# Gate rows written in 64 byte pieces, and a backward pass that gives engines and the DMA path one operation at a time

## The chip, the core and the metric

The kernel runs on one core of one Trainium2 chip. The core has TensorE (PE, matrix products into PSUM banks), VectorE (DVE), ScalarE (ACT), GpSimd (POOL) and SyncE (SP). In this kernel SP issues the loads, POOL most stores to scratch in DRAM. The metric is the device time of one execution in microseconds (us), lower is better. Before the change it was 880.47 us, the median of three runs (879.82 to 882.48).

## The reference

An input x of 2,048 tokens by 640 features goes through two branches, and a gate per token mixes them:

```
g = sigmoid((x * gate_w).sum(-1))              # one number per token
a = Cr @ (x @ Wre.T) - Ci @ (x @ Wim.T)        # Fourier mixing over features and tokens
b = mish(x @ w1 + b1) @ w2                     # 640 -> 1728 -> 640
out = g * a + (1 - g) * b
```

All is float32.

## The kernel before

**Products.** Every float32 operand is split into a high part (rounded by ACT) and a low part (the rest, by DVE), and a product of two operands is three matmuls: high by high, high by low, low by high (`mm3`). On top of that, the large products are cut into 2 x 2 blocks and done with seven block products in place of eight, with sums of blocks before and after them. A class `Problem` does one such product in three steps, `first`, `second` and `third`. The sums of inputs, and the sums that bring results out of PSUM, are DVE `tensor_tensor` operations (`tt`, L259); ACT copies between PSUM and SBUF (`copy`, L268); operands of 128 x 512 are split at L286 (ACT) and L287 (DVE), weight blocks at L280 and L281; the matmul itself is L292.

**Stages.** The work runs in this order on PE:

1. `seq`, four problems q0 to q3: x by the cosine and the sine matrix over tokens. Results `u0` to `u9` go to DRAM.
2. `hid`, two problems: u by the feature matrices `wd_re`, `wd_im`. Results, multiplied by g, go to DRAM as `y`.
3. `dense`: x by w1, mish, multiplied by 1 − g for half of the tokens, to DRAM as `act`.
4. `fin`, two problems: act by w2, plus y, to the output.

Some problems put partial sums of their first step aside in DRAM (`ps`, `ph`, `po`) and load them again in the second. Loads are L246, stores L255.

**The gate.** `gates()` (recorded in the third seq problem) loads `gate_w` to all partitions and x in 16 tiles of 128 tokens by 640. One DVE operation per tile multiplies and sums over the features (L746) and leaves a column of `gcol`, a tile of 128 partitions by 16 columns. ACT takes the sigmoid (L750), and DVE makes `qcol` = 1 − g (L751). Later stages need g and 1 − g along the free dimension, the same on all partitions. So both tiles go out to DRAM as rows of 2,048 numbers, `grow` and `qrow` (L753), and pieces of 512 of a row are loaded again, broadcast to 128 partitions (`f<-grow`, `f<-qrow`, L246). In the row of before token k · 128 + p stands in column k of partition p, so neighbours in the row lie on different partitions and the store goes out in pieces of one number.

**The order.** No engine's order is written by hand. Every operation is first recorded in a `Graph`, with its engine, what it reads and writes, and a modelled duration. The order of PE is that of recording, and each matmul's time `op.at` is its place in it times 0.2267 us (`MM`). `wants()` gives every other operation a latest time, `want`: a pass backwards over the operations takes, for each, the earliest `want` of those that need it, less its own duration and 0.15 us (`HOP`). Operations that bring results out of PSUM (`prompt`) also have a time from a pass forward, and the earlier one holds. `run()` then simulates the engines and writes out, on each engine, the ready operation with the earliest `want` for which buffers are to be had. Five pools hand out the buffers: 8 PSUM banks, 10 operand pairs R, 18 tiles FS (`f`), 6 wide tiles X (`x`), 26 weight pairs W (`w`). A buffer is kept free for operations of earlier `want` (`v.ask`). SP and POOL share one modelled DMA path of 385 GB/s with a delay of 1.95 us. What comes out is a fixed order per engine; on the chip an engine goes through its list and stops at each operation until what it needs is there. That holds for SP too: a load that waits for a free tile, or for data in DRAM to land, stops every load behind it.

Of the kernel before, what the change touches and what calls it, by code (L numbers as in the profile page):

```python
# [14 lines left out]
S, D, F = 2048, 640, 1728  # L15
P = 128
N = 512
TG = S // N
KS = S // P
# [5 lines left out]
NR, NFS, NX, NW = 10, 18, 6, 26  # L25
MM = 0.2267
HOP, PROMPT, LATER, AHEAD = 0.15, 2.0, 8.0, 5.0


class Val:  # L30
# [15 lines left out]
class Graph:  # L46
# [35 lines left out]
    def wants(self):  # L82

        for op in self.ops:
            for d in op.deps:
                d.after.append(op)
            if op.engine == "PE":
                op.ends = op.at + op.took
                op.want = op.at
                continue  # L90
            op.prompt = op.psum or not op.fills and any(d.prompt and d.engine in ("ACT", "DVE") for d in op.deps)
            if op.prompt:
                op.ends = max([d.ends for d in op.deps if d.prompt or d.engine == "PE"], default=0) + op.took
                op.want = op.ends + (PROMPT if op.psum else LATER)
        for op in reversed(self.ops):
            late = min([a.want for a in op.after], default=1e9) - op.took - HOP
            op.want = late if op.want is None else min(op.want, late)

    def run(self, pools, rate, delay):

        self.wants()
        for op in self.ops:
            for v in op.vals:
                if v.pool and (v.ask is None or op.want < v.ask[0]):
                    v.ask = op.want, op.n, id(v)
        for p in pools:
            p.asks = sorted({v.ask for op in self.ops for v in op.vals if v.pool is p})
            p.soon = sorted({v.ask for op in self.ops if op.prompt for v in op.vals if v.pool is p and v.ask[1] == op.n})
        missing = {op.n: len(op.deps) for op in self.ops}
        free = {e: 0.0 for e in ("PE", "ACT", "DVE", "SP", "POOL")}  # L110
        ready = {e: [] for e in free}
        pe = [op.n for op in self.ops if op.engine == "PE"][::-1]
        for op in self.ops:
            if not missing[op.n]:
                insort(ready[op.engine], (op.want, op.n))
        events, now, left, dma = [], 0.0, len(self.ops), 0.0

        def granted(op, blocked):
            for v in op.vals:
                if v.pool and v.t is None:  # L120
                    if v.pool in blocked:
                        return False
                    p, n = v.pool, bisect_left(v.pool.asks, v.ask)
                    if not op.prompt:
                        n += bisect_left(p.soon, (v.ask[0] + AHEAD,)) - bisect_left(p.soon, v.ask)
                    if len(p.free) <= n:
                        blocked.add(v.pool)
                        return False
            return True

        while left:
            began = False
            for e, line in ready.items():
                if free[e] > now + 1e-9 or not line:
                    continue
                if e == "PE":
                    i = next((i for i, x in enumerate(line) if x[1] == pe[-1]), None)
                    if i is not None and not granted(self.ops[pe[-1]], set()):
                        i = None
                else:  # L140
                    blocked = set()
                    i = next((i for i, x in enumerate(line) if granted(self.ops[x[1]], blocked)), None)
                if i is None:
                    continue
                op = self.ops[line.pop(i)[1]]
                if e == "PE":
                    pe.pop()
                for v in op.vals:
                    if v.pool and v.t is None:
                        v.pool.asks.remove(v.ask)  # L150
                        if v.ask in v.pool.soon:
                            v.pool.soon.remove(v.ask)
                        v.t = v.pool.free.pop(0)
                op.emit()
                free[e] = now + op.hold
                if e in ("SP", "POOL"):
                    dma = max(now + delay, dma) + op.took - delay
                    end = dma + 0.1
                else:
                    end = now + op.took + 0.03  # L160
                heapq.heappush(events, (end, op.n))
                left -= 1
                began = True
            if began:
                continue
            times = [t for e, t in free.items() if t > now + 1e-9 and ready[e]]
            if events:
                times.append(events[0][0])
            assert times, ("stuck", left, pe and self.ops[pe[-1]].at, [(p.name, len(p.free)) for p in pools])
            now = max(now, min(times))  # L170
            while events and events[0][0] <= now + 1e-9:
                op = self.ops[heapq.heappop(events)[1]]
                for v in op.vals:
                    v.left -= 1
                    if not v.left and v.pool:
                        p = v.pool
                        p.free.append(v.t)
                        if p.heir and not p.asks:
                            p.heir.free += [p.part(t) for t in p.free]
                            p.free = []  # L180
                for a in op.after:
                    missing[a.n] -= 1
                    if not missing[a.n]:
                        insort(ready[a.engine], (a.want, a.n))
# [8 lines left out]
def fnet_mish_gate(ctx: ExitStack, tc: tile.TileContext, xn, xt, c_re, c_im, wd_re, wd_im,  # L193
                   w1a, w1b, b1a, b1b, w2, gw, out):
    nc = tc.nc
# [9 lines left out]
    R = Pool("r", [pair(f"r{i}", N) for i in range(NR)])  # L205
# [31 lines left out]
        return G.add("ACT", emit, r, w, took, took - 0.096)  # L237

    def dma(queue, emit, r, w, size):
        return G.add(queue, emit, r, w, 1.95 + size / 385e3, 0.605 if queue == "SP" else 1.0)  # L240

    ISSUE = {"SP": nc.sync, "POOL": nc.gpsimd}

    def load(pool, src, of=None, rows=P, cols=N, queue="SP"):
        v = Val(pool)
        dma(queue, lambda: ISSUE[queue].dma_start(v.t[:rows, :cols], src() if callable(src) else src),  # L246
            whole(of) if of else [], whole(v), rows * cols * 4)
        return v
# [113 lines left out]
    class Problem:  # L362
# [154 lines left out]
        def end(self):  # L517
            (p0, p1), t, h = self.b, self.t1, N // 2
            f, g = Val(FS), Val(FS)
            copy(f, p0)  # L520
            self.finish(2, t, f, "SP")
            for eng, c in (("ACT", slice(0, h)), ("DVE", slice(h, N))):
                def emit(c=c, eng=eng):
                    if eng == "ACT":
                        nc.scalar.activation(g.t[:, c], p1.t[:, c], AF.Copy)
                    else:
                        nc.vector.tensor_copy(g.t[:, c], p1.t[:, c])
                (act if eng == "ACT" else dve)(emit, whole(p1), [(g, eng)], h)

                def send(c=c, eng=eng):  # L530
                    o = out[3 * P:4 * P, t * N + c.start:t * N + c.stop]
                    (nc.scalar if eng == "ACT" else nc.sync).dma_start(o, g.t[:, c])
                G.add("ACT" if eng == "ACT" else "SP", send, [(g, eng)], [], 2.3, 0.1)

    once = {}

# [204 lines left out]
    def gates():  # L741

        wide = load(X, gw.partition_broadcast(P), cols=D)
        for k in range(KS):
            x = load(X, xn[k], cols=D)
            dve(lambda k=k, x=x: nc.vector.scalar_tensor_tensor(  # L746
                x.t, x.t, 1.0, wide.t, op0=OP.mult, op1=OP.mult, accum_out=gcol.t[:, k:k + 1]),
                whole(x, wide), whole(x) + [(gcol, k)], D, 0.1)
        cols = [(gcol, k) for k in range(KS)]
        act(lambda: nc.scalar.activation(gcol.t, gcol.t, AF.Sigmoid), cols, cols, KS)  # L750
        dve(lambda: nc.vector.tensor_scalar(qcol.t, gcol.t, -1.0, 1.0, op0=OP.mult, op1=OP.add), cols, whole(qcol), KS)  # L751
        for c, row, r in ((gcol, grow, cols), (qcol, qrow, whole(qcol))):
            dma("SP", lambda c=c, row=row: nc.sync.dma_start(row.t.rearrange("o (k p) -> p (o k)", p=P), c.t),  # L753
                r, whole(row), 1 << 18)
        act(lambda: nc.scalar.preload_act_table_set("mish"), cols, whole(table), 0, 1.0)

# [54 lines left out]
    for p in ou:  # L811
        p.second(fin.low)
        p.third()
    G.run([psum, R, FS, X, W], 385.0, 1.95)


# [40 lines left out]
```

## Time and profile before

| | |
|---|---|
| median of 3 runs | 880.47 us |
| the profiled execution | 882.19 us, of it the span 880.4 us |
| PE busy | 861.5 us, 98% of the span, 3,772 matmuls |
| DVE busy | 677.8 us, 77%, 1,213 instructions |
| ACT busy | 461.6 us, 52%, 849 instructions |
| POOL busy | 69.3 us, 8% |
| moved by DMA | 203.50 MB in 107,071 packets, mean 231 GB/s |
| packets under 512 B | 16,640 |

How to read the views: a row of a table of groups or a timeline names the engine, the line of the kernel, the operation and `out<-in` by the program's names without buffer numbers (`f<-u` is a load of a u block into an FS tile). Times are us from the start of the span. `SPq` is SP's queue of issued DMAs; the time to landing is from the issue until the data is there. "Waited for" tables name the waiting engine and line, then what ended the wait, then the total, the number of waits and the longest. The windows view has one row per stretch of time: its length, busy time and count of PE, weight loads, DVE, ACT and POOL, the granted clock of PE (1.00 is full), the busy share of the 16 DMA engines, and GB/s. A digit in the DMA line is the busy share of one fortieth of the window in tenths.

### The profile page before, as it was taken

To read this page: it belongs to the slowest core of one execution; us is meant where nothing else is said; L and a number is where in the kernel's file an instruction comes from. 1 tells how busy PE (TensorE), PEld (TensorE's weight loads), DVE (VectorE), ACT (ScalarE), POOL (GpSimd) and SP (SyncE) were. 2 spreads that over 40 slices of the span, in tenths; PEclk is the share of its full clock that TensorE was granted. 3 is DMA by queue.
4 is the path that set the end of the run, shared out by engine and by line. 5 is a ranking of instruction groups with operands and counts; after the bars stand their busy time and mean duration, and the time that the engine had idled before them with its cause. 6 is when DMAs were issued, how large, how long until landed. Compare 5 with 4: busy or idle time off the path is not lost.

```text
span 880.4 us, 11973 instructions
## 1 busy us (share of the span) xinstructions
PE 861.5 (98%) x3772; PEld 710.2 (81%) x3772; DVE 677.8 (77%) x1213; ACT 461.6 (52%) x849; POOL 69.3 (8%) x132
## 2 busy tenths in 40 slices
PE   9999999999999999999995999999999999999998
PEld 7888888888888888888884888888888888887786
DVE  7899957866785667997976999924666997739891
ACT  7675535535453445674552576745655755522541
POOL 0000001002000200011001102111111100000000
PEclk9999999999999999999997999999999999999999
DMA  9796939555954755559975959565444687526943
GB/s 319 273 337 223 324 123 366 181 204 164 346 191 146 254 202 179 196 200 367 374 193 154 373 179 338 211 222 190 146 159 188 214 304 265 199 77 221 366 160 119
DMA packets 107071, 203.50 MB, mean 231 GB/s; under 512 B 16640, under 2 KB 19072, under 8 KB 107008
## 3 DMA queue, kind: packets, MB, share of 16 engines
q1 hardware_dynamic: 96752, 169.57, 56.5%
q0 software_dynamic: 10112, 33.04, 10.0%
q8 instruction: 29, 0.48, 0.2%
q14 instruction: 34, 0.28, 0.1%
q10 hardware_dynamic: 144, 0.13, 0.0%
HBM read 164.40 MB, written 38.29 MB: 230 GB/s over the span
## 4 chain that ended last, share of the span: by engine, by line
PE 85%; DMA 6%; DVE 6%; ACT 1%; issue 1%; SPq 0%; ACTq 0%; DVEq 0%
PE ps L292 85%; DMA f<-u 4%; DVE f L259 3%; DMA x<-in_xn_dram 1%; DMA f<-po 1%; DVE x L746 1%; DVE x L259 0%; DVE r8l L287 0%; ACT f L268 0%; DVE r9l L287 0%; DMA out_dram<-f 0%; ACT r8h L286 0%; DVE r1l L287 0%; DVE r5l L287 0%; ACT r1h L286 0%
## 5 line engine op out<-in xcount | busy, mean ns | idle before, releaser
L259 DVE TENSOR_TENSOR f<-f,f 128x512 f32<-128x512 f32 x316 | 211.8, 686 | 19.6 <-DMA f<-u 15.3
L268 ACT ACTIVATE f<-ps 128x512 f32<-128x512 f32 x129 | 74.5, 595 | 40.2 <-PE ps L292 35.1
L259 DVE TENSOR_TENSOR f<-ps,f 128x512 f32<-128x512 f32 x92 | 59.8, 684 | 38.4 <-PE ps L292 38.3
L255 POOL DMA_DIRECT2D u<-f x40 | 21.5, 540 | 321.6 <-DVE f L259 310.3
L286 ACT ACTIVATE r4h<-f 128x512 fp32r<-128x512 f32 x40 | 25.2, 629 | 37.9 <-PE ps L292 20.2
L286 ACT ACTIVATE r6h<-f 128x512 fp32r<-128x512 f32 x40 | 25.3, 631 | 37.5 <-PE ps L292 17.3
L286 ACT ACTIVATE r1h<-f 128x512 fp32r<-128x512 f32 x39 | 24.5, 629 | 33.0 <-PE ps L292 17.7
L550 ACT ACTIVATE f<-f,b1s 128x512 f32<-128x512 f32 x36 | 25.6, 722 | 28.2 <-DVE f L259 28.1
L286 ACT ACTIVATE r3h<-f 128x512 fp32r<-128x512 f32 x41 | 25.8, 629 | 26.0 <-PE ps L292 13.1
L286 ACT ACTIVATE r2h<-f 128x512 fp32r<-128x512 f32 x41 | 25.8, 628 | 25.4 <-PE ps L292 16.6
L286 ACT ACTIVATE r9h<-f 128x512 fp32r<-128x512 f32 x42 | 26.4, 629 | 23.1 <-PE ps L292 10.7
L255 POOL DMA_DIRECT2D act<-f x52 | 28.2, 542 | 131.0 <-DVE f L259 65.3
L286 ACT ACTIVATE r5h<-f 128x512 fp32r<-128x512 f32 x40 | 25.1, 629 | 25.3 <-PE ps L292 13.3
L287 DVE TENSOR_TENSOR r3l<-f,r3h 128x512 fp32r<-128x512 f32 x41 | 28.2, 688 | 11.6 <-ACT r3h L286 11.2
L286 ACT ACTIVATE r8h<-f 128x512 fp32r<-128x512 f32 x39 | 24.5, 629 | 24.0 <-PE ps L292 14.8
L286 ACT ACTIVATE r0h<-f 128x512 fp32r<-128x512 f32 x40 | 25.1, 629 | 22.1 <-PE ps L292 13.9
L287 DVE TENSOR_TENSOR r9l<-f,r9h 128x512 fp32r<-128x512 f32 x42 | 28.9, 688 | 9.6 <-ACT r9h L286 9.0
L287 DVE TENSOR_TENSOR r0l<-f,r0h 128x512 fp32r<-128x512 f32 x40 | 27.5, 688 | 11.4 <-ACT r0h L286 11.3
L287 DVE TENSOR_TENSOR r2l<-f,r2h 128x512 fp32r<-128x512 f32 x41 | 28.2, 688 | 10.0 <-ACT r2h L286 9.7
L287 DVE TENSOR_TENSOR r8l<-f,r8h 128x512 fp32r<-128x512 f32 x39 | 26.8, 688 | 11.3 <-ACT r8h L286 11.0
L287 DVE TENSOR_TENSOR r6l<-f,r6h 128x512 fp32r<-128x512 f32 x40 | 27.5, 688 | 9.7 <-ACT r6h L286 9.4
L287 DVE TENSOR_TENSOR r5l<-f,r5h 128x512 fp32r<-128x512 f32 x40 | 27.5, 688 | 9.2 <-ACT r5h L286 8.9
(1827 smaller groups left out, 2650.0 us busy)
## 6 DMA issues: line engine op xcount, KB each, us to landing
f<-in_c_re_dram SPq DMA_DIRECT2D x128, 256.0 KB, 4.9
f<-in_c_im_dram SPq DMA_DIRECT2D x128, 256.0 KB, 3.5
f<-act SPq DMA_DIRECT2D x84, 256.0 KB, 5.2
f<-u SPq DMA_DIRECT2D x80, 256.0 KB, 5.7
act<-f POOLq DMA_DIRECT2D x52, 256.0 KB, 2.9
f<-in_xt_dram SPq DMA_DIRECT2D x44, 256.0 KB, 4.4
u<-f POOLq DMA_DIRECT2D x40, 256.0 KB, 5.2
x<-in_xn_dram SPq DMA_DIRECT2D x25, 320.0 KB, 5.7
```

Source lines behind the costliest of these rows:

```text
L255: dma(queue, lambda: ISSUE[queue].dma_start(d.t, v.t[:rows]), whole(v), whole(d), rows * N * 4)
L259: dve(lambda: nc.vector.tensor_tensor(o.t[rows, x], a.t[rows, y], b.t[rows, z], op=op), whole(a, b), whole(o), n)
L268: act(lambda: nc.scalar.activation(o.t, a.t, AF.Copy, scale=scale), whole(a), whole(o))
L286: act(lambda: nc.scalar.activation(r.t[0][:, :N], src.t[:, :N], AF.Copy), whole(src), [(r, 0)])
L287: dve(lambda: nc.vector.tensor_tensor(r.t[1][:, :N], src.t[:, :N], f32(r.t[0][:, :N]), op=OP.subtract), whole(src) + [(r, 0)], [(r, 1)])
L292: G.add("PE", lambda: nc.tensor.matmul(bank.t, w.t[wn][:, k * P:k * P + P], x.t[xn_][:, :N], start, stop, skip_group_check=True), [(w, (k, ...
L550: act(lambda: nc.scalar.activation(o.t[rows], src.t[rows], AF.Mish, **more), whole(src, table) + whole(b1s) * bias, whole(o), more=0.1)
L746: dve(lambda k=k, x=x: nc.vector.scalar_tensor_tensor(x.t, x.t, 1.0, wide.t, op0=OP.mult, op1=OP.mult, accum_out=gcol.t[:, k:k + 1]), whol ...
```

## The change

Two parts.

The gate's x is read so that partition p has the 16 tokens p · 16 to p · 16 + 15, one per tile; then the 16 columns of a partition are neighbours in the row, and the store of a row has 128 pieces of 16 numbers (64 bytes). The number of instructions is the same.

```
+        tokens = xn.rearrange("k p d -> (k p) d").rearrange("(p k) d -> k p d", k=KS)
         for k in range(KS):
-            x = load(X, xn[k], cols=D)
+            x = load(X, tokens[k], cols=D)
...
-            dma("SP", lambda c=c, row=row: nc.sync.dma_start(row.t.rearrange("o (k p) -> p (o k)", p=P), c.t),
+            dma("SP", lambda c=c, row=row: nc.sync.dma_start(row.t.rearrange("o (p k) -> p (o k)", k=KS), c.t),
```

The backward pass of `wants()` is replaced. The new one keeps a heap of operations all of whose successors are done, and takes the latest first. On ACT and on DVE, and on the DMA path that SP and POOL share, operations may not overlap: each must end before the one taken ahead of it begins (`back`). A matmul's `want` is `op.at` alone. The model of the DMA path becomes 370 GB/s with a delay of 2.2 us, and a transfer holds the path for its bytes' time (`op.moves`). Where an operation takes two buffers of one pool, its `v.ask` is set so that both count from the time of the later (the loop added to `run`).

```
+DELAY, RATE = 2.2, 370e3
...
-        for op in reversed(self.ops):
+        back, todo, line = {}, {op.n: len(op.after) for op in self.ops}, []
+
+        def reached(op):
             late = min([a.want for a in op.after], default=1e9) - op.took - HOP
-            op.want = late if op.want is None else min(op.want, late)
-
-    def run(self, pools, rate, delay):
+            if op.want is not None:
+                late = op.at if op.engine == "PE" else min(op.want, late)
+            heapq.heappush(line, (-late, -op.n))
+        for op in self.ops:
+            if not op.after:
+                reached(op)
+        while line:
+            late, n = heapq.heappop(line)
+            op, late = self.ops[-n], -late
+            if op.engine == "PE":
+                op.want = late
+            else:
+                e, held = ("DMA", op.moves) if op.engine in ("SP", "POOL") else (op.engine, op.hold)
+                ends = min(late + op.took, back.get(e, 1e9))
+                op.want, back[e] = ends - op.took, ends - held
+            for d in op.deps:
+                todo[d.n] -= 1
+                if not todo[d.n]:
+                    reached(d)
...
+        for op in self.ops:
+            for v in op.vals:
+                if v.pool and v.ask[1] == op.n:
+                    also = [u.ask[0] for u in op.vals if u.pool is v.pool and u is not v]
+                    if also:
+                        v.ask = min(v.ask, (max(also), op.n, id(v)))
...
-                    dma = max(now + delay, dma) + op.took - delay
+                    dma = max(now + DELAY, dma) + op.moves
...
-        return G.add(queue, emit, r, w, 1.95 + size / 385e3, 0.605 if queue == "SP" else 1.0)
+        op = G.add(queue, emit, r, w, DELAY + size / RATE, 0.605 if queue == "SP" else 1.0)
+        op.moves = size / RATE
+        return op
...
-                G.add("ACT" if eng == "ACT" else "SP", send, [(g, eng)], [], 2.3, 0.1)
+                G.add("ACT" if eng == "ACT" else "SP", send, [(g, eng)], [], 2.3, 0.1).moves = 0.4
```

The matmuls and their order, the number of instructions of every kind, and the pools stay as they are.

More of the change, by code (lines that the diff above doesn't have):

```diff
@@ L94, in wants, with run @@
                 op.want = op.ends + (PROMPT if op.psum else LATER)
-        for op in reversed(self.ops):
+        back, todo, line = {}, {op.n: len(op.after) for op in self.ops}, []
+        def reached(op):
             late = min([a.want for a in op.after], default=1e9) - op.took - HOP
-            op.want = late if op.want is None else min(op.want, late)
-    def run(self, pools, rate, delay):
+            if op.want is not None:
[17 more added lines that the diff above has]
+                    reached(d)
+    def run(self, pools):
         self.wants()
@@ L813, in fnet_mish_gate @@
         p.third()
-    G.run([psum, R, FS, X, W], 385.0, 1.95)
+    G.run([psum, R, FS, X, W])
 def kernel(**inputs):
```

## The prediction

> **What bounds the kernel now.** I read the page's first rows, then the waits of PE (TensorE), then windows around its largest wait, then the queues in those windows. Page, first rows:
>
> ```profile
> span 880.4 us, 11973 instructions
> ## 1 busy us (share of the span) xinstructions
> PE 861.5 (98%) x3772; PEld 710.2 (81%) x3772; DVE 677.8 (77%) x1213; ACT 461.6 (52%) x849; POOL 69.3 (8%) x132
> ```
>
> PE is busy for all but 880.4 − 861.5 = 18.9 us. The matmuls and their order do not change, so the change can win only what PE stands idle or runs slowly, and can lose any amount. The waits of PE (us in total, times, longest):
>
> ```profile
> PE ps L292 <- DVE f L259: 10.3, 1, 10.3
> PE ps L292 <- ACT ps L268: 2.2, 3, 1.5
> ```
>
> One wait holds 10.3 us: a PSUM bank that DVE has not yet emptied. Windows around the large wait (width; busy us and count of PE, PEld, DVE, ACT, POOL; granted clock; DMA share; GB/s):
>
> ```profile
> 442.00:457.00 15.00, 15.00 (x68) 12.40 (x67) 10.59 (x19) 8.66 (x16) 0.00 (x0) 1.00 0.72 163
> 457.00:470.50 13.50, 13.50 (x60) 10.88 (x58) 5.71 (x12) 1.60 (x3) 0.00 (x0) 1.00 0.66 120
> 470.50:480.80 10.30, 0.02 (x1) 0.01 (x1) 9.38 (x17) 4.65 (x8) 0.76 (x2) 0.69 0.48 178
> 480.80:485.00 4.20, 4.17 (x10) 3.32 (x11) 4.20 (x8) 0.60 (x1) 2.95 (x6) 0.53 0.79 276
> ```
>
> PE starves at 470.5 because DVE was short of input before it: 5.71 us busy of 13.5. After the wait PE runs on at a clock of 0.53. What DVE waited for between 442 and 476, and what the DMA engines did from 440 to 472 (40 slices of 0.8 us):
>
> ```profile
> DVE f L259 <- DMA f<-u: 12.9, 4, 7.1
> ```
>
> ```profile
> DMA  9999999950259443379888799982131366585989
> GB/s 377 398 387 394 381 394 242 87 2 0 20 41 69 26 38 26 32 129 312 335 271 182 156 320 394 303 56 22 1 0 8 31 61 36 28 69 82 318 318 402
> DMA packets 6996, 5.40 MB, mean 169 GB/s; under 512 B 4443, under 2 KB 4443, under 8 KB 6994
> ```
>
> Twice the path falls from nearly 400 GB/s to a few tens for some 9 us, and of 6,996 packets 4,443 are small. SP's issues show which they are (start, issue us; the rows between are left out), and the table of issues gives the landing times (KB each, median us):
>
> ```profile
> 442.10 0.37 SPq L753 DMA_DIRECT2D grow<-gcol  x1
> ...
> 457.44 0.37 SPq L753 DMA_DIRECT2D qrow<-qcol  x1
> ```
>
> ```profile
> f<-u SPq DMA_DIRECT2D x80, 256.0 KB, 5.7
> ...
> out_dram<-f SPq DMA_DIRECT2D x1, 128.0 KB, 1.9
> b1s<-in_b1a_dram SPq DMA_DIRECT2D x1, 6.5 KB, 5.2
> ...
> grow<-gcol SPq DMA_DIRECT2D x1, 8.0 KB, 11.9
> qrow<-qcol SPq DMA_DIRECT2D x1, 8.0 KB, 11.1
> ```
>
> Each gate row (8 KB, 2,048 pieces of 4 B, 4,096 of the small packets) takes 11 to 12 us. The chain that ended last has the loads issued right behind the rows:
>
> ```profile
> 442.77 12.22 DMA f<-u
> ...
> 457.86 13.29 DMA f<-u
> ```
>
> They take 12.22 and 13.29 us against a median of 5.7: 6.5 and 7.6 late, 14.1 together. That is about DVE's 12.9 us of waiting, which becomes PE's 10.3.
>
> **The change part by part.**
>
> *Rows in 64 B pieces.* Removed per row: 1,920 of 2,048 pieces; the instruction count stays. No row of before shows 128 pieces of 64 B going out. Nearest is b1a's load, 128 pieces of 52 B: 5.2 us. Ends: 1.9 (the 128 KB store of the quiet end) and 11.9 (no gain). I take 5.2; by it a piece costs (11.9 − 5.2)/1,920 = 3.5 ns, and 128 of them 0.4 us: no load behind is held measurably.
>
> The Trainium skill, "DMA: Bandwidth & Descriptors" (Specifications), says that pieces under 512 B miss line rate because the engine reads, modifies and writes; 64 B is still under that, as 4 B was. If that alone made the row slow, it would take 11.9 us again and the sum would be the third rival's; the section on one DMA's anatomy fits about 2.0 us plus bytes by 436 GB/s, an estimate of 2.0 us for 8 KB, and with it the sum below stands.
>
> *What goes with it.* DVE's 12.9 us disappear if the loads come at their usual 5.7. DVE's release of the bank, which let PE go on at 480.8, then comes at about 480.7 − 12.9 = 467.8, before the 470.5 at which PE wants the bank. Slack: 2.7 us, not much. Gain 10.3 us. With it goes the slow clock: nine matmuls of 0.43 us in place of 0.2267 us (starts of 480.82 to 484.77 below, less the first one's 0.57), 9 × 0.2 = 1.8, call it 1.9.
>
> ```profile
> 480.82 0.76 PE L292 MATMUL ps<-r4h,w11h 128*128 128x512 f32 x1 [10.30 <-DVE f L259]
> ...
> 484.77 0.39 PE L292 MATMUL ps<-r5h,w21h 128*128 128x512 f32 x1
> ```
>
> The Trainium skill, "TensorE: Matmul & The Clock Gate" (Part 1), has the clock halve after an idle window of about 3.4 us and come back after about as long busy; the 0.53 of 480.8 to 485 agrees. By it a wait that shrinks under 3.4 us would cost its own length only, and one that stays above would keep the 1.9.
>
> *Gathering the gate's x rows.* Partition p now takes tokens 16p to 16p+15: still 128 pieces of 2,560 B, from addresses 40,960 B apart rather than adjacent. Sixteen loads, taken at nothing; were each 1 us of path longer, 16 us would fall into 396 to 442, where the path is full (next fence), and the sums of u would be late.
>
> *The planner.* PE's list is the same. In the written-out orders 932 of DVE's 1,195 operations, 522 of ACT's 849, 448 of SP's 643 and 7 of POOL's 128 change place. Three moves matter. (a) Five loads of `wd_re` (320 KB, tops of the hidden stage), which SP issues at 78 to 83 us, go out at about 370 to 384, with their splits on ACT and DVE. (b) Eight loads of u go ahead of the gate's x loads, from about 398–412 to 360–383. (c) The grow row's first read stands directly behind its store, so SP stops until the row has landed; behind it wait two u loads, the qrow store and the next reads. Before, three loads went in between, and SP stopped 4.2 us:
>
> ```profile
> SPq L246 <- DVE w14l L281: 19.9, 3, 10.4
> ...
> SPq L246 <- DMA grow<-gcol: 4.2, 1, 4.2
> ```
>
> With a landing of 5.2 SP stops about 5 us from some 443, and is free at 448; before, the same loads were issued from 449 to 455. So (c) costs nothing, and with 11.9 us it would cost what before paid. For (a) and (b), windows with more and less room:
>
> ```profile
> 346.00:396.00 50.00, 50.00 (x223) 41.38 (x222) 48.00 (x99) 35.47 (x74) 2.78 (x6) 1.00 0.63 215
> 396.00:442.00 46.00, 46.00 (x204) 38.07 (x203) 40.73 (x80) 23.99 (x45) 4.20 (x8) 1.00 1.02 371
> ...
> 504.00:577.00 73.00, 73.00 (x324) 60.47 (x323) 71.91 (x144) 51.38 (x105) 11.95 (x22) 1.00 0.71 250
> 577.00:592.50 15.50, 15.50 (x71) 12.82 (x70) 0.69 (x1) 5.69 (x9) 2.16 (x4) 1.00 0.60 227
> ```
>
> Five tops are 1.6 MB: 4.4 us at 371 GB/s, into a window where the path is used to 0.63; eight u loads are 2 MB, taken out of the one that is full. The splits add some 5 × 0.7 = 3.5 us to DVE where it is busy for 48.0 of 50. Giving each operation of the new order its duration in the trace of before, and PE its times there, DVE stays some 12 us ahead of what PE needs in that window, so 3.5 are hidden; if that cover were gone they would cost 3.5. From 504 to 577 DVE is full (71.91 of 73) and then has 14.8 us free, so it is only just in time: small waits may appear. I allow +1.0 for them, with ends 0 and 5 (the 2.7 us of slack used up twice over).
>
> *The end of the kernel.* Near 810 PE waits for ACT to copy partial sums into banks, and ACT for the load that brings them (`po`, the aside of the last stage):
>
> ```profile
> 806.51 5.92 DMA f<-po
> 812.45 0.61 ACT ps L268
> ```
>
> That is most of the 2.2 us of the ACT wait above, and with small gaps about 3. The `po` loads now stand three and one places earlier on SP, ahead of output stores: at about 0.5 us a place, 1.5 and 0.5 earlier. I take −1.2, ends −3 and 0.
>
> Sum on the profiled execution (882.19 us, of which 1.8 lie around the span): 882.2 − 10.3 − 1.9 − 1.2 + 1.0 = 869.8. It ran 1.72 above the median of 880.47, so on the median 868.1; I say 868.5.
>
> **The rivals.**
> - *Stall partly kept.* Without the 12.9 us DVE has 2.7 us to spare; a few late loads (SP's stop, reordered DVE work) keep a wait of 3 to 9 us. For it: PE would have to be fed by DVE without a break from 504 to 577. Against: the loads that are late today have no other cause in the trace. Time: 868.5 + 3 to + 9 = 871.5 to 877.5.
> - *A new wait for X tiles: slower.* The five tops share the six X tiles with the gate's loads, and SP stops for a free one: 10.4 us once above, before the u loads. If one such stop stood ahead of u loads that PE needs, with the longest stop of the whole run, 14.3 us (next fence), uncovered, it costs 14.3 + 1.9 of slow clock: 882.2 − 12.4 + 16.2 = 886.0, on the median 884.3. It decides from about 13 us of uncovered stop. Against: the u loads were put earlier by some 30 us.
>
> ```profile
> SPq L246 <- DVE x L259: 44.7, 19, 14.3
> ```
>
> - *64 B pieces as slow as 4 B ones.* The price would lie in the row of 8 KB, not in its pieces. Then the 12.9 us stay, and only the end's gain is left: 880.5 − 1.2 + 1.0, about 880. For it: no row shows such a store. Against: b1a's 5.2 us.
>
> **How the numbers follow.** The measurement tells about 0.3% (2.6 us) from no change: below 877.8 is faster, above 883.1 slower. Stall gone (866 to 871.5; best case 865.3, all stalls but start and finish gone): 0.62, with 0.02 below it. Partly kept: 0.22. As slow as before: 0.05. Slower: 0.09. Faster is 0.62 + 0.02 + 0.21 = 0.85, same 0.06, slower 0.09. The likeliest case's own range is 866 to 871.5; to hold 8 in 10 it must reach through most of the second: 866 to 876.5.
>
> **What would show it.** Right: both rows land in about 5 us; no f<-u load near them takes over 8; packets under 512 B fall by 3,840; DVE's wait for f<-u from 442 to 476 under 3 us; PE's 10.3 us wait and the 0.53 clock gone; PE busy some 859.5, the span near 868. Wrong: rows at 11 us; a stop of SP for an X tile from 365 to 396 with PE waiting behind it; a PE wait for DVE between 448 and 577 over 3 us; new waits near 810.

## The result and the profile after

The changed kernel takes 868.27 us (median of 4 runs, 867.66 to 868.47) beside 881.22 us for the kernel before (median of 4, 879.82 to 882.48). The ratio is 0.9852, with a 95% interval of 0.9834 to 0.9870: faster by 1.5%. The prediction was 868.5, with a range of 866.0 to 876.5. The profiled execution took 868.39 us with a span of 866.6.

The first rows of the page of the changed kernel, and its waits of PE (the line numbers of the changed file are 29 higher from L246 on: L259 became L288, L292 became L321, L268 became L297):

```profile
span 866.6 us, 11980 instructions
...
PE 859.3 (99%) x3772; PEld 709.0 (82%) x3772; DVE 679.0 (78%) x1213; ACT 463.1 (53%) x849; POOL 69.7 (8%) x132
```

```profile
PE ps L744 <- DVE r9l L742: 2.0, 1, 2.0
PE ps L321 <- DVE r1l L316: 0.4, 1, 0.4
PE ps L321 <- ACT ps L297: 0.3, 1, 0.3
```

The wait of 10.3 us is gone, and nothing of its size took its place; the longest that is left is the start. PE idles 866.6 − 859.3 = 7.3 us instead of 18.9. The windows around the place show PE without a break and at full clock, and DVE fed: 11.38 us busy of 13 between 457 and 470, against 5.71 of 13.5 before.

```profile
442.00:457.00 15.00, 15.00 (x68) 12.43 (x67) 13.49 (x26) 8.85 (x14) 0.00 (x0) 1.00 0.76 261
457.00:470.00 13.00, 13.00 (x60) 10.74 (x58) 11.38 (x21) 5.29 (x9) 2.49 (x5) 1.00 0.33 118
470.00:474.00 4.00, 4.00 (x19) 3.33 (x18) 4.00 (x7) 0.95 (x2) 2.90 (x6) 1.00 0.92 307
```

The two rows land in 2.8 and 3.5 us (KB, us to landing). DVE's longest waits from 442 to 476 are no longer for u loads:

```profile
grow<-gcol SPq DMA_DIRECT2D x1, 8.0 KB, 2.8
qrow<-qcol SPq DMA_DIRECT2D x1, 8.0 KB, 3.5
```

```profile
DVE r8l L316 <- ACT r8h L315: 1.4, 1, 1.4
DVE x L288 <- DMA x<-in_w1a_dram: 1.2, 1, 1.2
```

PE's order is the same in both kernels, so the start of one and the same matmul can be set against itself. These are four matmuls of the changed kernel, all from PE's timeline:

```profile
470.00 0.39 PE L321 MATMUL ps<-r4h,w11h 128*128 128x512 f32 x1
...
472.04 0.39 PE L321 MATMUL ps<-r5h,w12h 128*128 128x512 f32 x1
...
797.31 0.50 PE L321 MATMUL ps<-r5h,w11h 128*128 128x512 f32 x1
...
807.25 0.50 PE L321 MATMUL ps<-r1l,w22h 128*128 128x512 f32 x1 [0.38 <-DVE r1l L316]
```

Before, the same ones start at 480.82 and 484.77 (shown in the prediction) and at:

```profile
811.81 0.49 PE L292 MATMUL ps<-r5h,w21h 128*128 128x512 f32 x1 [1.55 <-ACT ps L268]
...
821.05 0.51 PE L292 MATMUL ps<-r1l,w22h 128*128 128x512 f32 x1 [0.23 <-DVE r1l L287]
```

The lead of the changed kernel is 10.8 us at the first, 12.7 at the second, 14.5 at the third and 13.8 at the last, and 13.8 is the difference of the spans. So: 0.3 us at the start of the kernel (at 20 us PE already has this lead) and 10.5 at the wait, 1.9 from the slow clock, 1.8 at the wait near 810, of which 0.7 is given back in small waits just after.

### The profile page after: what moved, and what is told of

Read it like the earlier page. It is cut to its first block, busy times and chain, and to the rows that moved or that the text cites. A ratio compares the mean times of both kernels' runs of the same rounds, so it can differ in the third digit from the quotient of the medians.

```text
span 866.6 us, 11980 instructions
## 1 busy us (share of the span) xinstructions
PE 859.3 (99%) x3772; PEld 709.0 (82%) x3772; DVE 679.0 (78%) x1213; ACT 463.1 (53%) x849; POOL 69.7 (8%) x132
## 3 DMA queue, kind: packets, MB, share of 16 engines
q0 software_dynamic: 10112, 33.04, 10.3%
## 4 chain that ended last, share of the span: by engine, by line
PE 96%; DVE 1%; DMA 1%; ACT 1%; issue 0%; ACTq 0%; DVEq 0%
PE ps L321 96%; DVE f L288 1%; DMA x<-po 1%; PE ps L744 0%; DMA out_dram<-f 0%; DVE x L288 0%; ACT ps L297 0%; ACT r5h L315 0%; DVE r9l L316 0%; DVE r7l L316 0%; ACT r4h L315 0%; ACT r9h L315 0%; ACT r3h L315 0%; DVE r1l L316 0%; ACT r6h L315 0%
## 5 line engine op out<-in xcount | busy, mean ns | idle before, releaser
L288 DVE TENSOR_TENSOR f<-f,f 128x512 f32<-128x512 f32 x311 | 209.1, 685 | 10.7 <-DMA f<-u 3.5
L288 DVE TENSOR_TENSOR f<-ps,f 128x512 f32<-128x512 f32 x101 | 66.0, 685 | 43.3 <-PE ps L321 43.0
L297 ACT ACTIVATE f<-ps 128x512 f32<-128x512 f32 x128 | 74.9, 595 | 38.9 <-PE ps L321 30.4
L316 DVE TENSOR_TENSOR r7l<-f,r7h 128x512 fp32r<-128x512 f32 x39 | 26.8, 688 | 12.8 <-ACT r7h L315 12.5
L315 ACT ACTIVATE r6h<-f 128x512 fp32r<-128x512 f32 x39 | 24.5, 629 | 22.7 <-PE ps L321 16.4
L315 ACT ACTIVATE r7h<-f 128x512 fp32r<-128x512 f32 x39 | 24.5, 629 | 22.6 <-PE ps L321 16.1
L316 DVE TENSOR_TENSOR r0l<-f,r0h 128x512 fp32r<-128x512 f32 x40 | 27.5, 688 | 10.5 <-ACT r0h L315 10.2
L315 ACT ACTIVATE r4h<-f 128x512 fp32r<-128x512 f32 x37 | 23.3, 629 | 21.4 <-PE ps L321 20.9
```

What stands on the lines that cost most here:

```text
L288: dve(lambda: nc.vector.tensor_tensor(o.t[rows, x], a.t[rows, y], b.t[rows, z], op=op), whole(a, b), whole(o), n)
L297: act(lambda: nc.scalar.activation(o.t, a.t, AF.Copy, scale=scale), whole(a), whole(o))
L315: act(lambda: nc.scalar.activation(r.t[0][:, :N], src.t[:, :N], AF.Copy), whole(src), [(r, 0)])
L316: dve(lambda: nc.vector.tensor_tensor(r.t[1][:, :N], src.t[:, :N], f32(r.t[0][:, :N]), op=OP.subtract), whole(src) + [(r, 0)], [(r, 1)])
```

## The experiments

"Before" is the kernel before, run beside each on the same chip. On the chips of the experiments it took 884 to 886 us, not 881, so ratios are given, and kernels are compared that ran on one chip.

**Each part alone.** The rows alone: the kernel before, with the first diff of the change and no other, so with the order of before on every engine.

> Only the rows change (128 pieces of 64 B); the planner and with it the order on every engine are those of before. If the rows carry the gain: both rows land in 3 to 4 us as in the changed kernel, DVE's 12.9 us of waiting for u loads and PE's 10.3 us wait go, with them the slow clock: 880.5 to 881.2 less 12.4 (10.5 + 1.9) is about 868.5, and the last 1 us, from the end near 810, stays: PE still waits there 2 us for ACT. If the new order carries it (loads put ahead of the rows): time stays within 3 us of 881, PE's wait of 7 us or more stays.

Measured: 870.54 us (869.69 to 871.17), ratio 0.9839 (0.9823 to 0.9854). PE's waits and the rows' landing:

```profile
PE ps L715 <- DVE r9l L713: 2.0, 1, 2.0
PE ps L292 <- ACT ps L268: 1.7, 3, 1.0
```

```profile
grow<-gcol SPq DMA_DIRECT2D x1, 8.0 KB, 5.0
qrow<-qcol SPq DMA_DIRECT2D x1, 8.0 KB, 1.4
```

PE's 10.3 us wait for DVE is gone with the order untouched; its wait for ACT near 800 stays. The profiled execution took 869.69 us, 12.5 less than the profiled one of before (882.19), where 12.4 were expected; the median is 2 us above the 868.5 that was expected.

The planner alone: the changed kernel with the two old row lines.

```
-        tokens = xn.rearrange("k p d -> (k p) d").rearrange("(p k) d -> k p d", k=KS)
-            x = load(X, tokens[k], cols=D)
+            x = load(X, xn[k], cols=D)
-            dma("SP", ... row.t.rearrange("o (p k) -> p (o k)", k=KS), c.t),
+            dma("SP", ... row.t.rearrange("o (k p) -> p (o k)", p=P), c.t),
```

> Only the planner changes; the rows go out in 2,048 pieces of 4 B. If the rows carry the gain: both rows take 11 to 12 us, SP stops some 11 us behind the grow store because the row's first read stands directly behind it, u loads are late, PE waits 8 to 16 us between 450 and 490: 877 to 887, so no gain or a loss. If the new order carries it: 868 to 872, no PE wait over 3 us. The end near 810 gains its 1 us either way.

Measured: 884.71 us (883.18 to 888.72), ratio 1.0003 (0.9990 to 1.0015): no difference. The stall is back as two waits of PE, 12.6 us together, and the rows are slow:

```profile
PE ps L321 <- DVE f L288: 6.8, 1, 6.8
PE ps L321 <- DVE r2l L316: 5.8, 1, 5.8
```

```profile
grow<-gcol SPq DMA_DIRECT2D x1, 8.0 KB, 10.9
qrow<-qcol SPq DMA_DIRECT2D x1, 8.0 KB, 13.7
```

So the rows carry the gain, and the new order by itself does not avoid the stall. SP's stop behind the grow store is real here: the row is issued at 441.58 and its first read, directly behind it, at 452.51. With nothing else issued, this run also shows the row by itself (windows; the last two columns are the DMA share and GB/s):

```profile
441.50:447.00 5.50, 5.50 (x26) 4.56 (x25) 5.50 (x11) 5.47 (x10) 0.00 (x0) 1.00 0.78 150
447.00:452.50 5.50, 5.50 (x26) 4.57 (x25) 4.09 (x7) 2.03 (x4) 0.00 (x0) 1.00 0.00 0
```

For the last 5.5 us before it lands the DMA engines show no work at all. What passes in them the profile does not show.

**What makes a row slow.** Three kernels keep the order of before and change the rows alone: 512 of 16 B, 1,024 of 8 B, and 2,048 of 4 B whose 16 neighbours in a row come from one partition. The first (the second has a=8, k=2):

```
+        tokens = xn.rearrange("k p d -> (k p) d").rearrange("(a p k) d -> a k p d", a=4, k=4)
-            x = load(X, xn[k], cols=D)
+            x = load(X, tokens[k // 4, k % 4], cols=D)
-            ... nc.sync.dma_start(row.t.rearrange("o (k p) -> p (o k)", p=P), c.t),
+            ... nc.sync.dma_start(row.t.rearrange("o (a p k) -> p (o a) k", a=4, k=4), c.t.rearrange("p (a k) -> p a k", a=4)),
```

> As the rows alone, but each row goes out in 512 pieces of 16 B. If a piece has a price (11.5 us for 2,048 and 3.2 us for 128 give 4.3 ns each): landing in about 4.8 us, no PE wait over 3 us, 868.5 to 871. If the price lies in the row being written in parts below some size, whatever their number: landing nearer 11 us and a PE wait of 7 to 10 us, 878 to 882.

> As the rows alone, each row in 1,024 pieces of 8 B; 2,048 pieces landed in about 11.5 us, 512 in about 4, 128 in about 3.2. If every piece has the same price (4.3 ns): about 7 us a row, loads behind it 3 to 4 us late, a PE wait of 0 to 3 us, 870 to 873. If the price sets in above some number of pieces: under 5 us and 868.5 to 871, or 10 us and more and 877 to 882.

The third, from the rows alone:

```
-            dma("SP", ... row.t.rearrange("o (p k) -> p (o k)", k=KS), c.t),
-                r, whole(row), 1 << 18)
+            def halves(c=c, row=row):
+                to, of = row.t.rearrange("o (p j i) -> i p (o j)", p=P, i=2), c.t.rearrange("p (j i) -> i p j", i=2)
+                for i in range(2):
+                    nc.sync.dma_start(to[i], of[i])
+            dma("SP", halves, r, whole(row), 1 << 18)
```

> The rows alone, but each row goes out as two stores of 1,024 pieces of 4 B, so 2,048 pieces as in the kernel before; what differs from before is that the 16 neighbours of every 64 B of a row come from one partition, not from 16. If the number of pieces has the price: a row lands 9 to 12 us after its first store, PE waits 7 to 11 us, 878 to 882 (with before at 880.5 to 881.2). If the price lies in many partitions writing into the same 64 B: landing in 3 to 6 us, no PE wait over 2 us, 868 to 871.

The landing of grow and qrow in the three, in this order (16 B, 8 B, 4 B from one partition; in the last, of each half of a row; below it PE's longest wait there):

```profile
grow<-gcol SPq DMA_DIRECT2D x1, 8.0 KB, 5.1
qrow<-qcol SPq DMA_DIRECT2D x1, 8.0 KB, 2.8
```

```profile
grow<-gcol SPq DMA_DIRECT2D x1, 8.0 KB, 7.6
qrow<-qcol SPq DMA_DIRECT2D x1, 8.0 KB, 6.9
```

```profile
grow<-gcol SPq DMA_DIRECT2D x2, 4.0 KB, 13.2
qrow<-qcol SPq DMA_DIRECT2D x2, 4.0 KB, 12.7
```

```profile
PE ps L292 <- DVE f L259: 14.9, 1, 14.9
```

| pieces per row | mean landing, us | time, us | ratio to before (95%) |
|---|---|---|---|
| 128 of 64 B (rows alone) | 3.2 | 870.54 | 0.9839 (0.9823 to 0.9854) |
| 512 of 16 B | 4.0 | 870.10 | 0.9833 (0.9817 to 0.9849) |
| 1,024 of 8 B | 7.3 | 870.82 | 0.9840 (0.9818 to 0.9861) |
| 2,048 of 4 B (before: landing in its first profile, time beside the first two rows) | 11.5 | 884.64 | 1 |
| 2,048 of 4 B, neighbours from one partition | 13.0 | 887.98 | 1.0046 (1.0028 to 1.0063) |

The landing goes with the number of pieces; neighbours from one partition do not help. That kernel's wait of 14.9 us and its 887.98 lie above what either expectation gave (7 to 11 us, 878 to 882 with before at 881, which took 884.3 here), so the pieces cost rather more there than was thought. As a row has 8 KB throughout, the pieces get smaller as they get more. That 4 B pieces are not slow by their size alone is seen in a load of before, `in_b1b`, which has 64 of them:

```profile
b1s<-in_b1b_dram SPq DMA_DIRECT2D x1, 0.2 KB, 4.4
```

From 1,024 to 2,048 pieces one costs (11.5 − 7.3)/1,024 = 4.1 ns, close to the 4.3 that was expected over the whole span; from 128 to 512 it is (4.0 − 3.2)/384 = 2.1 ns, within what two rows of one kernel differ by. The time does not follow in proportion. At 7.3 us the loads behind are late enough for DVE to wait 3.2 us, and PE waits 0.5:

```profile
DVE f L259 <- DMA f<-u: 3.2, 2, 3.0
```

```profile
PE ps L292 <- DVE f L259: 0.5, 1, 0.5
```

So DVE's slack holds here, as it was worked out from the trace of before: 2.7 us of cover, 3.2 of delay, 0.5 of stall.

**Another queue.** The kernel before, with its 4 B rows issued by ACT:

```
-            dma("SP", lambda c=c, row=row: nc.sync.dma_start(row.t.rearrange("o (k p) -> p (o k)", p=P), c.t),
-                r, whole(row), 1 << 18)
+            G.add("ACT", lambda c=c, row=row: nc.scalar.dma_start(row.t.rearrange("o (k p) -> p (o k)", p=P), c.t),
+                  r, whole(row), 2.63, 0.1)
```

> The kernel before with its 4 B rows, but both stores are issued by ACT's queue and not by SP's; the list of the other engines changes little. If the loads are late because they stand behind the pieces in SP's queue: rows still 11 us or more, u loads near 441 to 470 at their usual 5 to 7 us, PE's wait under 4 us, 869 to 874. If the pieces hold up the DMA engines whatever the queue: u loads beside them still take 10 us or more, PE waits 7 to 12 us, 878 to 884.

Measured: 880.38 us, ratio 0.9940 (0.9920 to 0.9961), but the runs reach from 877.66 to 886.13, and the profiled one is that of 886.13. In it the rows take longer still, the u loads on SP's queue beside them (440 to 472) take 10.9 us at the median (9.1 in before in the same stretch), and PE waits 12.6:

```profile
f<-u SPq DMA_DIRECT2D x13, 256.0 KB, 10.9
...
grow<-gcol ACTq DMA_DIRECT2D x1, 8.0 KB, 13.2
qrow<-qcol ACTq DMA_DIRECT2D x1, 8.0 KB, 16.4
```

```profile
PE ps L292 <- DVE f L259: 12.6, 1, 12.6
```

So it is not their place behind the pieces in SP's queue that makes the loads late: what the pieces hold up is shared by both queues. The median lies in the range of this second expectation (878 to 884). The profiled run had a mean clock of 0.990, the other three 0.996. Why they differ, and so why this kernel gains 0.6%, stays open.

**The planner's part.** The changed kernel and the rows alone again, on one chip, and between them the changed kernel with the old backward pass (its loop `for op in reversed(self.ops)` as in the diff of the change; the new DMA model, the asking times and the 64 B rows stay):

> The changed kernel again, beside the rows alone on one chip. If the planner's part is worth the 1.0 to 1.3 us at the end that the traces show: about 1.2 us less than the rows alone, ratio to before near 0.985. If it is worth nothing: within 0.5 us of the rows alone.

> The rows alone (64 B pieces, order of before), beside the changed kernel on one chip. ACT's wait of PE near 800 stays at 1 to 2 us in total; if the end is where the planner's part pays, 1.2 us more than the changed kernel; otherwise the same.

> The changed kernel with the old backward pass; the new model of the DMA path, the new asking times and the 64 B rows stay. In its order the two po loads stand where they stood before. If the backward pass gives the end's gain: 1 us or more over the changed kernel, PE waits 1 us or more for ACT near 800. If the DMA model or the asking times give it: the time of the changed kernel.

| | time, us | range | ratio to before (95%) |
|---|---|---|---|
| changed kernel | 868.40 | 868.08 to 868.84 | 0.9821 (0.9799 to 0.9842) |
| rows alone | 870.09 | 869.81 to 872.49 | 0.9845 (0.9824 to 0.9865) |
| changed, old backward pass | 874.20 | 872.30 to 875.78 | 0.9881 (0.9860 to 0.9903) |

The planner's part is worth 1.7 us on top of the rows; the two ranges do not touch. The new backward pass is needed for it: with the old one, the other parts make the kernel slower than the rows alone, by 4.1 us. It is not enough by itself, as the last experiment shows. The waits of PE with the old pass:

```profile
PE ps L301 <- ACT f L277: 2.8, 1, 2.8
PE ps L301 <- ACT ps L277: 2.1, 3, 1.5
```

The 2.1 is mostly the wait near 800, which the rows alone have too. The 2.8 is at 420 us, where ACT brings a bank out late behind a late u load. The profiled runs of the rows alone wait there 0 and 0.5 us, the three profiled runs of the changed kernel not at all, so the new order took away a place with no slack as well. How the wait near 800 went is seen in SP's issue of the `po` load and PE's start of the matmul that needs it. Rows alone:

```profile
793.26 0.49 SPq L246 DMA_DIRECT2D f<-po  x1
```

```profile
799.15 0.50 PE L292 MATMUL ps<-r5h,w21h 128*128 128x512 f32 x1 [1.04 <-ACT ps L268]
```

Changed kernel (its matmul at 797.31 is above, and waits for nothing):

```profile
790.52 0.32 SPq L275 DMA_DIRECT2D x<-po  x1
```

PE wants it at 799.15 − 1.04 = 798.11 in the one and at 797.31 in the other, so the load goes out 4.9 us ahead of the need in the first and 6.8 ahead in the second. ACT, which waits for it in the first, goes on at 798.49, 5.2 us after the issue, so 4.9 could not cover it; in the changed kernel it takes 5.5, and 6.8 can.

Last, the changed kernel with `DELAY, RATE = 1.95, 385e3`:

> The changed kernel with the old figures of the modelled DMA path (1.95 us and 385 GB/s); backward pass, asking times and 64 B rows stay. If the new pass with its asking times gives the planner's 1.7 us: within 1 us of the changed kernel, no PE wait for ACT over 0.5 us near 420 and near 800. If the new figures matter: 1 us or more slower, one of the two waits back.

> The changed kernel beside the old figures on one chip: 868 to 869, no PE wait over 0.5 us but for the start.

Measured on one chip: 869.93 us (868.96 to 870.54) with the old figures, 868.47 (868.23 to 868.65) with the new ones, so the figures are worth 1.5 us: the second of the two expectations. With the old ones PE waits 0.9 us near 800, 0.9 between 431 and 560 and 0.5 between 560 and 780. Without the new figures, as without the new pass, most or all of the planner's 1.7 us is gone; the parts do not add up one by one, and the asking times were not run apart. No version beat the changed kernel.

## Why the prediction was right

*The bound.* Right. PE's one large wait was the thing to win, with the slow clock behind it; beside them 1.1 us at the end and 0.3 at the start moved.

*The rows.* Right in kind and in size: 5.2 us a row were taken; 2.8 and 3.5 came, and up to 5.0 with the old order. Small packets were to fall by 3,840 and fell from 16,640 to 12,800. The piece price of 3.5 ns, from a load at another time of the kernel, measured 4.1.

*What goes with it.* The bank was to come free at 467.8. It came free with the first of the two DVE operations that start at 466.28:

```profile
466.28 1.28 DVE L288 TENSOR_TENSOR f<-ps,f 128x512 f32<-128x512 f32 x2
```

Half of 1.28 us on, that is 466.9, and PE wants it at 470.00: 3.1 us of slack where 2.7 were forecast. Gain 10.5 for 10.3, and 1.9 for 1.9 at the clock.

*The gate's x.* Right: taken at nothing; the 16 loads of 320 KB from `xn` that are issued from 375 to 440 land in 5.9 us at the median in both kernels.

*The planner's stop of SP (c).* Right that it costs nothing with fast rows: SP waited 2.4 us there instead of 4.2, and 5 were allowed. With 4 B rows it was to cost "what before paid", and the planner alone ended at ratio 1.0003.

*The end.* Right in its working, and in the net size of 1.1 us for 1.2. In the traces the two `po` loads are the 581st and 583rd of SP's 643 issues before, and the 578th and 582nd after: three places and one earlier, as forecast. For this the prediction took 1.5 and 0.5 us. Beside the rows alone the first goes out 1.9 us more ahead of its need, as shown above, and the second 0.5. The wait itself gave 1.8 us; the 0.7 lost in small waits just after was in no term.

*The allowance of +1.0 for new waits.* This term was wrong. DVE was to be only just in time from 504 to 577; no wait of PE is seen in the changed kernel between 431 and 780, although DVE is as full there as before (69.42 us of 70 from 490 to 560). Taking the measured terms in the place of the forecast ones, 0.3 + 10.5 + 1.9 + 1.1 = 13.8 for 12.4, gives the 868.39 of the profiled execution; the sum had 869.8 for it. The 868.5 for the median came so near because 1.7 us were taken off for the place of the profiled run of before among its runs, which the changed kernel, whose runs lie within 1 us, does not have. Two misses of 1.4 us and 1.7 us nearly cancelled: the mechanism held, but that the forecast came within 0.3 us of the result is luck.

*The rivals.* The stall kept in part: not seen, though the 8 B rows show that it begins at about 7 us a row. The new wait for X tiles: not seen; SP's longest wait between 350 and 470 is 6.4 us, for a y block. (The 14.3 us of this rival is the longest stop of its own row; SP's waits before also have one of 26.9 us, for DVE at L281.) The 64 B pieces as slow as 4 B: refuted by the landing. Nor does the rule of the Trainium skill ("DMA: Bandwidth & Descriptors", Specifications), by which pieces under 512 B miss line rate, tell the cases apart: in these runs 16 B pieces cost as little as 64 B ones, and 4 B ones about three times as much. The estimate of 2.0 us for 8 KB comes from a fit that the Trainium skill gives, in the section of the same page on the anatomy of one DMA, for DMAs issued by GpSimd; these rows go out from SP, and in 64 B pieces they took 1.4 to 5.1 us.

*The clock rule of the Trainium skill.* The prediction used "TensorE: Matmul & The Clock Gate" (Part 1) to say that a wait under 3.4 us would cost its own length only. The runs differ. In the kernel with the old backward pass, PE idles 1.49 and 0.29 us near 804, and the next 3.5 us pass at a clock of 0.52:

```profile
802.00:805.30 3.30, 1.56 (x6) 0.99 (x7) 3.27 (x6) 1.75 (x3) 0.00 (x0) 1.00 1.06 385
805.30:808.80 3.50, 3.50 (x10) 2.72 (x9) 0.78 (x3) 0.63 (x1) 0.00 (x0) 0.52 1.04 396
```

Before, 1.55 and 0.35 us of idle at the same place had no such sequel. So a short wait can cost its length and about 1.6 us more (eight starts, 805.27 to 808.66, in 3.39 us in place of 8 × 0.2267), and need not.

Where the idle time falls may decide it. In each trace the granted clock changes at times that lie whole multiples of 3.41 us apart (474.48 and 484.71 before, three of them; 805.28 and 808.69 with the old pass, one). Windows laid on these times, first with the old pass and then before:

```profile
801.87:805.28 3.41, 1.63 (x7) 0.97 (x7) 3.38 (x6) 1.75 (x3) 0.00 (x0) 1.00 1.07 387
805.28:808.69 3.41, 3.41 (x10) 2.63 (x9) 0.69 (x3) 0.63 (x1) 0.00 (x0) 0.50 1.05 398
```

```profile
808.98:812.39 3.41, 1.86 (x9) 1.25 (x7) 2.69 (x5) 2.19 (x4) 0.00 (x0) 1.00 1.03 387
812.39:815.80 3.41, 3.06 (x14) 2.20 (x13) 1.92 (x4) 0.91 (x2) 0.00 (x0) 1.00 1.07 388
```

With the old pass both waits fall into one stretch, which leaves PE 1.63 us busy; before, they fall into two, 1.86 and 3.06. Where the limit lies is not shown: with the rows on ACT's queue a stretch with 1.89 us busy (813.73 to 817.14) was followed by a halved clock as well.

## What to carry to other kernels

Price a small transfer by its pieces, not its bytes alone: here 8 KB in 2,048 pieces took 11 to 16 us, held up the loads beside it, on its own queue or another, and cost 12 us on an engine far from it, while the same 8 KB in 512 pieces or fewer took 1.4 to 5.1. When an engine starves, look at what the DMA path moves in that window. Here it fell to a few tens of GB/s while most of the packets were small, and choosing which token goes to which partition made the pieces neighbours at no cost that the traces show. The planner's better due times paid in a few places where slack was near nothing; they were worth 1.7 us beside the rows' 12, and parts of them without the rest cost time.

## What was not expected of the hardware

- Of the 10.9 us that a lone 4 B row took to land, the DMA engines showed no work in the last 5.5.
- The kernel before took 880.5 to 881.2 us in the first comparisons and 884.3 to 885.8 beside the experiments, while the changed kernel took 868.27, 868.40 and 868.47. The mean clock of before beside the experiments was 0.990 to 0.994, that of the changed kernel 0.999 to 1.000. What varies may hang on the 4 B rows, which landed in 10.9 to 16.4 us in the profiles that have them, and on the halved clock behind the stall; this was not shown.
- Idle of 1.8 us in two pieces was followed by a halved clock in one kernel, and idle of 1.9 us in two pieces by none in another.
